# Gate and value by seven block products on 768 tokens, in three passes over combined weights

## The chip, the cores and the metric

The kernel runs on one core of one Trainium2 chip. The metric is the device time of one execution in microseconds. The engines are named as in the profile: PE (TensorE, matrix products), DVE (VectorE), ACT (ScalarE), POOL (GpSimd) and SP (SyncE, which here issues most transfers). SBUF is the memory on the chip that the engines work in, PSUM the small memory into which PE adds up its products.

## What is computed

```python
# attention without softmax over positions: B=8, H=8, S=576, D=64, 128 features
def phi(x):
    proj = einsum('bhsd,df->bhsf', x, w_phi)
    proj = proj - max(abs(proj), axis=-1, keepdims=True)
    return concatenate([exp(proj), exp(-proj)], axis=-1)
q_p, k_p = phi(q), phi(k)
kv = einsum('bhsf,bhsd->bhfd', k_p, v);  z = sum(k_p, axis=2)
attn = einsum('bhsf,bhfd->bhsd', q_p, kv) / (einsum('bhsf,bhf->bhs', q_p, z)[..., None] + 1e-06)
x = attn.transpose(0, 2, 1, 3).reshape(4608, 512)
# RMS norm, then gate and value (512 -> 1536), then output (1536 -> 512)
xn = x / sqrt(mean(x * x, axis=-1, keepdims=True) + 1e-06) * rms_g
g = xn @ w_gate;  val = xn @ w_val
out = (g * (1.0 / (1.0 + exp(-g))) * val) @ w_out
```

The weights of gate, value and output come in 64-bit floating point and are decoded on the chip; all else is 32-bit.

## The kernel before

A product of 32-bit numbers is made of three: each operand is split into a high part (a cast on ACT to the type that PE takes, `fp32r`) and a low part (a subtraction on DVE or POOL, `_split`, lines 59 to 61), and high x high, high x low and low x high are added up in PSUM. So every operand of a product costs one cast and one subtraction, and most rows on DVE and POOL at line 61 are such subtractions; their names end in `l`, those of the casts in `h`.

The program runs in three stages, one after the other, with some overlap.

- Attention (to about 512 us of the profile) handles pairs of heads in a software pipeline, and writes the tokens of x to `xs` in the chip's main memory. In its pauses PE does *fill* units (line 474): the products of the first three (`J1`) of the twelve blocks of 128 hidden columns with tokens that are not yet normalised, since the norm is a factor of each token that can be multiplied in later. One unit is 12 matmuls of 128x288; there are 96, and their results are stored in `gvs`. Units that attention did not take run behind it.
- The gate and value stage (about 620 to 1066 us) works on blocks of 384 tokens, 12 of them (`NB`), and for each on the nine other hidden blocks (`JN`). `gv` (line 576) makes 12 matmuls of 128x384 for the gate into `fp` and 12 for the value into `gp` (line 588); `hidden` applies the silu on ACT and multiplies on DVE (line 573) and stores to `hs`. All weights stay in SBUF, split (`wg`, `wv`, and `fg`, `fv` for the fills). Beside it `prep` makes the norm of the next block (squares on ACT, sums on POOL, line 151, the reciprocal and the scaling on DVE, lines 160 and 162, the split of x into `xb`), `gv_raw` scales the fills' results by the norm (line 596), 24 pieces of `w_out` are decoded (lines 47 to 55), and `load_o` splits weights of the output stage.
- The output stage (1066 us to the end) already uses Strassen's scheme in Winograd's form: the product of two by two blocks with seven block products instead of eight. It runs in 18 groups of 256 tokens, 126 matmuls of 128x256 each (line 742, `omm`). `load_o` makes the seven weight combinations of each of six weight groups (`kp`) and splits them into `wh`, `wl`; `operands` makes the seven token combinations of the next group (`a11`, `a12`, `s1` to `s4`, `a22`) while PE works on the present one.

The order of instructions on each engine is set when the program is built, by a scheduler that orders by data dependencies and priorities; each engine runs its own list in order. Pieces of side work are put between matmuls by hand in the Python loops. Tiles are reused in turn, so an instruction that writes a tile waits for the readers of what stood there.

## Time and profile before

| what | value |
|---|---|
| median of 3 runs | 1335.12 us (1331.82 to 1335.24) |
| span of the profiled execution | 1337.6 us |
| PE, DVE, ACT, POOL busy | 1288.5, 885.0, 711.0, 605.5 us |
| moved by DMA | 197.22 MB, mean 147 GB/s |
| matmuls 128x384 of the gate and value stage | 2592 |

The times are device times of whole executions. The profile is of one further execution; an engine is busy while one of its instructions runs. The stages are told apart by the source lines of PE's matmuls: 474 for fills, 588 for gate and value, 742 for output.

### The profile page before, as it was taken

What the parts mean: (1) busy time and instruction counts of PE and PEld (TensorE: products, weight loads), DVE (VectorE), ACT (ScalarE), POOL (GpSimd) and SP (SyncE); (2) the same over time, 40 slices, a digit from 0 to 9 for tenths busy, and PEclk for the clock granted to TensorE, in tenths of its full rate; (3) what the DMA queues carried; (4) which work ended last, traced back from release to release, by engine and by line L of the source; (5) the groups of instructions that cost most, each with busy time, mean ns of one, the idle gap of its engine ahead of it and who ended that gap; (6) DMA issues with size and microseconds to landing.
All of it is one profiled execution on the core that took longest, in us unless ns stands there. A gap on an engine that the chain in (4) does not pass through costs nothing.

```text
span 1337.6 us, 25479 instructions
## 1 busy us (share of the span) xinstructions
PE 1288.5 (96%) x9396; PEld 1275.6 (95%) x9396; DVE 885.0 (66%) x1301; ACT 711.0 (53%) x1510; POOL 605.5 (45%) x568
## 2 busy tenths in 40 slices
PE   7989999999999896899999999999999999999998
PEld 7989899999999896899999999999999999999998
DVE  7899788778778773313456656655534498777784
ACT  5988877778778782434344344443333334434332
POOL 3766565555555570000233223233221078788684
PEclk9999999999999898999999999999999999999999
DMA  5555556566555434843454454554433534554451
GB/s 159 127 147 156 161 158 165 167 170 169 157 164 161 123 95 127 249 153 126 141 170 140 157 168 133 166 168 140 133 115 108 183 111 126 150 166 127 142 168 54
DMA packets 204524, 197.22 MB, mean 147 GB/s; under 512 B 69552, under 2 KB 186416, under 8 KB 204400
## 3 DMA queue, kind: packets, MB, share of 16 engines
q1 hardware_dynamic: 186448, 181.44, 45.2%
q10 hardware_dynamic: 17952, 14.16, 3.8%
q8 instruction: 74, 1.21, 0.4%
q14 instruction: 50, 0.41, 0.1%
HBM read 126.04 MB, written 69.50 MB: 146 GB/s over the span
## 4 chain that ended last, share of the span: by engine, by line
PE 57%; DMA 3%; DVE 1%; ACT 0%; issue 0%; POOL 0%; ACTq 0%; SPq 0%; DVEq 0%
PE fp L588 17%; PE gp L588 16%; PE gd L742 6%; PE gz L742 6%; PE gy L742 5%; PE fp L474 4%; PE fp L742 3%; DMA wc<-wvs 1%; DMA gvs<-fo 1%; DMA rc<-di 0%; PE sm L415 0%; DMA dd<-nd 0%; ACT fo L477 0%; POOL s2l L61 0%; DVE a12l L61 0%
## 5 line engine op out<-in xcount | busy, mean ns | idle before, releaser
L380 POOL TENSOR_TENSOR ql<-eq,qh 128x256 fp32r<-128x256 f32 x256 | 217.7, 882 | 67.3 <-issue 39.5
L588 PE MATMUL gp<-xb,wv 128*128 128x384 f32 x864 | 161.9, 334 | 0.8 <-ACT wv L60 0.8
L588 PE MATMUL fp<-xb,wg 128*128 128x384 f32 x864 | 161.0, 334 | 0.0
L573 DVE TENSOR_TENSOR h<-sl,gp 128x384 f32<-128x384 f32 x108 | 59.6, 552 | 144.2 <-PE gp L588 75.6
L588 PEld LDWEIGHTS gp<-xb,wv 128*128 128x128 f32 x864 | 150.7, 188 | 1.0 <-ACT wv L60 1.0
L571 ACT ACTIVATE sl<-fp 128x384 f32<-128x384 f32 x108 | 52.8, 489 | 185.6 <-PE fp L588 170.7
L588 PEld LDWEIGHTS fp<-xb,wg 128*128 128x128 f32 x864 | 150.7, 188 | 0.0
L54 POOL TENSOR_TENSOR wa<-raw,wa 128x192 f32<-128x192 f32 (+1 forms) x112 | 66.2, 613 | 162.2 <-issue 58.6
L351 PE MATMUL acc<-vm,ek 128*128 128x65 f32 x1024 | 131.8, 271 | 0.0
L315 DVE TENSOR_REDUCE mx<-pp 128x4 f32<-128x512 f32 (+1 forms) x160 | 100.6, 632 | 43.0 <-PE pp L313 41.5
L351 PEld LDWEIGHTS acc<-vm,ek 128*128 128x128 f32 x1024 | 128.1, 195 | 0.4 <-ACT ek L338 0.4
L151 POOL TENSOR_TENSOR ss<-ss,sq 128x384 f32<-128x384 f32 x36 | 37.6, 1044 | 160.6 <-ACT sq L150 160.6
L61 POOL TENSOR_TENSOR xb<-x,xb 128x1536 fp32r<-128x1536 f32 x12 | 42.5, 3540 | 132.3 <-ACT xb L60 124.6
L474 PE MATMUL fp<-xo,fg 128*128 128x288 f32 x576 | 92.8, 302 | 5.7 <-ACT fo L477 3.4
L376 ACT ACTIVATE qh<-sm 128x512 fp32r<-128x512 f32 (+1 forms) x192 | 97.3, 507 | 0.0
L474 PE MATMUL fp<-xo,fv 128*128 128x288 f32 x576 | 92.2, 300 | 4.4 <-ACT fo L477 4.4
L311 PE MATMUL pp<-wh,th 128*128 128x256 f32 x288 | 89.0, 310 | 2.7 <-DVE yr L318 2.1
L474 PEld LDWEIGHTS fp<-xo,fg 128*128 128x128 f32 x576 | 81.7, 190 | 7.4 <-ACT fo L477 4.4
L474 PEld LDWEIGHTS fp<-xo,fv 128*128 128x128 f32 x576 | 81.7, 190 | 5.1 <-ACT fo L477 5.1
L61 POOL TENSOR_TENSOR s2l<-st,s2h 128x768 fp32r<-128x768 f32 x18 | 43.5, 2419 | 95.0 <-ACT s2h L60 47.6
L375 ACT ACTIVATE eq<-sm 128x512 f32<-128x512 f32 x128 | 78.4, 612 | 14.1 <-PE sm L364 13.2
L313 PE MATMUL pp<-wh,tl 128*128 128x256 f32 x288 | 83.0, 298 | 1.8 <-DVE tl L61 1.8
(198 smaller groups left out, 3801.8 us busy)
## 6 DMA issues: line engine op xcount, KB each, us to landing
hs<-h SPq DMA_DIRECT2D x144, 192.0 KB
ht<-hs SPq DMA_DIRECT2D x18, 1536.0 KB
gvs<-fo SPq DMA_DIRECT2D x96, 144.0 KB
gvr<-gvs SPq DMA_DIRECT2D x36, 384.0 KB
rc<-di SPq DMA_DIRECT2D x32, 288.0 KB
x<-xs ACTq DMA_DIRECT2D x16, 576.0 KB
x<-xs SPq DMA_DIRECT2D x12, 768.0 KB
kt<-in_k_dram SPq DMA_DIRECT2D x32, 256.0 KB
```

The source lines that it names most:

```text
L54: nc.gpsimd.tensor_tensor(a[:, h], lf[:, h], a[:, h], ALU.mult)
L61: (lo_eng or nc.vector).tensor_tensor(lo, x, hi.bitcast(F32), ALU.subtract)
L311: nc.tensor.matmul(o, th[:, cs], wh, start=True, stop=False)
L313: nc.tensor.matmul(o, tl[:, cs], wh, start=False, stop=True)
L315: nc.vector.tensor_reduce(mx[:, 0:2 * m], pp[:, 0:2 * m], axis=AX.X, op=ALU.max, apply_absolute_value=True)
L351: nc.tensor.matmul(acc[:, sg, h], e[h][:, sg, j], vm[:, h, j], start=False, stop=(h == 1 and j == T0 - 1))
L375: nc.scalar.activation(ei[:, sg], yi, AF.Exp, scale=1.0 - 2.0 * sg)
L376: nc.scalar.activation(hi[:, sg], yi, AF.Exp, scale=1.0 - 2.0 * sg)
L380: nc.gpsimd.tensor_tensor(lo[:, sg, cs], ei[:, sg, cs], hi[:, sg, cs].bitcast(F32), ALU.subtract)
L474: nc.tensor.matmul(fp[:, 0:TF], w, xx[x][:, c], start=(i == 0), stop=(i == 3 * NC - 1))
L588: nc.tensor.matmul(gp[:, 0:T], w, e[:, c], start=(i == 0), stop=(i == 3 * NC - 1))
L742: nc.tensor.matmul(place[n], a[:, kp], w[:, o], start=(first and kp == 0 and i == 0), stop=(kp == KP - 1 and i == 2), skip_group_check=True)
```

## The change

Gate and value are put on the seven-product scheme. The left matrix has two rows of blocks, gate and value, and two columns, the halves of the 512 inner columns; the right matrix has the two halves of the inner columns and two blocks of 384 tokens. So one *pair* (`pair`) serves 768 tokens and one hidden block j with 7 products x 2 inner blocks x 3 = 42 matmuls of 128x384 (line 666 of the changed kernel) instead of 48. Several products are added up in the same PSUM bank (`gx` or `fp`, `gy`, `gz`); five additions on DVE that read PSUM (line 670) combine the rest.

- The tokens need seven combinations, split, for each 768 tokens (`load_x`), and the weights seven for each j (`load_w`). The split token combinations are large, so only two blocks of 768 are held (`xa`), and only four sets of weights (`wb`, `NW`). The stage therefore runs in three passes (`NS`) of two blocks, and in each pass all nine weight sets are loaded and split again; the first pass computes the combinations and stores them in `wcs`, the other two load them.
- Norms are made in pieces (`norm`) for each 384 tokens. The fills' results are scaled in `raw`, six at the end of attention on DVE, the others on POOL in the first two passes.
- Side work stands in two lists, `todo` and `soon`, of which `step` runs pieces between the products.
- The 24 decodings of `w_out` stand in the third pass. `load_o` moves as a whole behind the gate and value stage, and the first output group is computed weight group by weight group.
- The fills' weights lie in attention's memory, so all fills end before the stage begins, but for what overlaps at its edge.

The diff, cut to the parts that are spoken of:

```diff
+    def norm(hb):
+        d = {}
+        def square(c):
+            sq = xm.tile([128, T], F32, name="sq" if c else "ss")
+            nc.scalar.activation(sq, xin[hb][:, c], AF.Square)
+            if c == 0:
+                d["ss"] = sq
+            else:
+                nc.gpsimd.tensor_tensor(d["ss"], d["ss"], sq, ALU.add)
...
+            sh = xm.tile([128, T], F32R, name="sq")
+            sl = xm.tile([128, T], F32R, name="sl")
+            _split(nc, sh, sl, d["ss"], lo_eng=nc.gpsimd)
+            nc.tensor.matmul(sp, ones, sh, start=True, stop=False)
+            nc.tensor.matmul(sp, ones, sl, start=False, stop=True)
+            ris[hb] = xm.tile([128, T], F32, name="ri", bufs=2)
+            nc.scalar.activation(ris[hb], sp, AF.Sqrt, scale=1.0 / DM, bias=eps)
+        def inverse(c):
+            nc.vector.reciprocal(ris[hb][:, c:c + 128], ris[hb][:, c:c + 128])
+        def scaled(c):
+            x = xin[hb][:, c]
+            nc.vector.scalar_tensor_tensor(x, x, g[:, c:c + 1], ris[hb], ALU.mult, ALU.mult)
...
-                nxt = prep(0, x0, ps_f, "fp")
+                for p in norm(0) + norm(1):
+                    p()
...
+            eng.tensor_tensor(d["r"], d["r"], ris[hb].unsqueeze(1).broadcast_to([128, 2, T]), ALU.mult)
+        def done():
+            r = d["r"]
+            nc.scalar.activation(r[:, 0], r[:, 0], AF.Silu)
+            nc.vector.tensor_tensor(r[:, 0], r[:, 0], r[:, 1], ALU.mult)
+            nc.sync.dma_start(out=hsv[:, j, at], in_=r[:, 0])
...
+            for p in raw(n, j, lambda: wk.tile([128, 2, 512], F32, name="eq")[:, :, 0:T], nc.vector):
+                p()
...
-            gp = ps_g.tile([128, 512], F32, name="gp") if wi else ps_f.tile([128, T], F32, name="fp")
...
+    PG = 3
+    SB = 2
+    NS = NB // (2 * SB)
+    SG = JN // PG * SB
+    NW = 4
...
+    def load_w(n, a, t):
+        d = {}
+        def begin():
+            pool = wlast if n % NW == NW - 1 else wpool
+            d["w"] = wb[n] = pool.tile([128, 2, 7, 256], F32R, name=f"wb{n % NW}")
+        def combos():
+            sub = lambda o, x, y: nc.vector.tensor_tensor(o, x, y, ALU.subtract)
+            nc.vector.tensor_tensor(t[:, 0], a[:, 2], a[:, 3], ALU.add)
+            sub(a[:, 2], a[:, 0], a[:, 2])
+            sub(t[:, 1], t[:, 0], a[:, 0])
+            sub(t[:, 2], a[:, 1], t[:, 1])
+            nc.sync.dma_start(out=wcv[n][:, 0:4], in_=a)
+            nc.sync.dma_start(out=wcv[n][:, 4:7], in_=t)
+        def split(x, os, lo_eng):
+            _split(nc, d["w"][:, 0, os], d["w"][:, 1, os], x, lo_eng=lo_eng)
+        return ([combos] if n < JN else []) + [begin, lambda: split(a, slice(0, 4), nc.gpsimd),
+                                               lambda: split(t, slice(4, 7), nc.vector)]
...
+    def load_x(bk):
+        d = {}
+        b11, b12, b21, b22 = (xin[2 * bk + i][:, 2 * k:2 * k + 2] for k in range(2) for i in range(2))
+        sub = lambda o, a, b: nc.vector.tensor_tensor(o, a, b, ALU.subtract)
+        def combos():
+            d["x"] = ops[bk] = xops[bk % SB].tile([128, 2, 7, 2, T], F32R, name="xa")
+            d["t"] = t = [xtp.tile([128, 2, T], F32, name=f"t{i}") for i in range(2)]
+            sub(t[0], b12, b11)
+            sub(t[1], b22, t[0])
+            sub(b12, b22, b12)
+        def split(i, x, lo_eng):
+            _split(nc, d["x"][:, 0, i], d["x"][:, 1, i], x, lo_eng=lo_eng)
+        def fourth():
+            split(4, d["t"][0], nc.vector)
+            sub(d["t"][0], b21, d["t"][1])
+        return [combos, lambda: split(0, b11, nc.gpsimd), fourth, lambda: split(5, d["t"][1], nc.vector),
+                lambda: split(1, b21, nc.gpsimd), lambda: split(6, d["t"][0], nc.vector),
+                lambda: split(3, b22, nc.gpsimd), lambda: split(2, b12, nc.gpsimd)]
...
+    def pair(bk, j, w, behind, step):
+        x = ops[bk]
+        X = ps_f.tile([128, T], F32, name="fp") if j % 2 else ps_g.tile([128, 512], F32, name="gx")[:, 0:T]
+        Y, Z = (ps_g.tile([128, 512], F32, name="g" + n)[:, 0:T] for n in "yz")
+        place = {1: X, 2: X, 6: Y, 7: Y, 4: Y, 5: Z, 3: Z}
+        def mm(n):
             i = 0
-            pl = place(wi, j)
-            for c in range(NC):
-                a, al = pl[0][:, c], pl[1][:, c]
-                for w, e in ((a, xh), (a, xl), (al, xh)):
-                    nc.tensor.matmul(gp[:, 0:T], w, e[:, c], start=(i == 0), stop=(i == 3 * NC - 1))
+            for c in range(2):
+                for a, e in ((0, 0), (0, 1), (1, 0)):
+                    nc.tensor.matmul(place[n], w[:, a, WSIDE[n], c * 128:(c + 1) * 128], x[:, e, XSIDE[n], c],
+                                     start=(i == 0 and n in (1, 6, 5)), stop=(i == 5), skip_group_check=True)
                     i += 1
-            r.append(gp[:, 0:T])
-        hidden(bk, J1 + j, *r)
-    def gv_raw(bk, j):
-        r = wk.tile([128, 2, T], F32, name="gvr", bufs=1)
-        nc.sync.dma_start(out=r, in_=gvv[j][:, :, bk * T:(bk + 1) * T])
-        nc.vector.tensor_tensor(r, r, xb[bk][2].unsqueeze(1).broadcast_to([128, 2, T]), ALU.mult)
-        hidden(bk, j, r[:, 0], r[:, 1])
-    W11, W21, W22, WT1, WT2, WT3, WT4 = range(7)
+        add = lambda o, a, b: nc.vector.tensor_tensor(o, a, b, ALU.add)
+        s1 = wk.tile([128, T], F32, name="s1")
+        vr = wk.tile([128, 2, T], F32, name="vr")
+        u, h = (wk.tile([128, T], F32, name=n) for n in "uh")
+        first = lambda: tc.high_priority(AHEAD)
+        with first():
+            mm(1)
+            nc.scalar.copy(s1, X)
+        step()
+        with first():
+            mm(6)
+            add(u, Y, s1)
+        step()
+        with first():
+            mm(5)
+        step()
+        for piece in behind:
+            with first():
+                piece()
+            step()
+        with first():
+            mm(2)
+            nc.scalar.activation(h, X, AF.Silu)
+        step()
+        with first():
+            mm(7)
+            add(vr[:, 1], Y, s1)
+            add(vr[:, 1], Z, vr[:, 1])
+        step()
+        def fourth():
+            mm(4)
+            add(vr[:, 0], Y, s1)
+        def third():
+            mm(3)
+            add(u, Z, u)
+            nc.scalar.activation(u, u, AF.Silu)
+            nc.vector.tensor_tensor(vr[:, 0], vr[:, 0], h, ALU.mult)
+            nc.vector.tensor_tensor(vr[:, 1], vr[:, 1], u, ALU.mult)
+            nc.sync.dma_start(out=hsv[:, J1 + j, 2 * bk * T:2 * (bk + 1) * T], in_=vr.rearrange("p a t -> p (a t)"))
+        return fourth, third
...
+    decs = [keep_o(i, j * 128, i * CH) for j in range(NJ) for i in range(DM // CH)]
...
+    for t in range(NS * SG):
+        s, u = divmod(t, SG)
+        gi, b = divmod(u, SB)
+        bk = s * SB + b
+        new = []
+        if t == 0:
+            new += raws(2) + raws(3)
+        if s and u == 0:
+            new += load_x(bk + 1)
+        if s + 1 < NS:
+            hb = 2 * SB * (s + 1) + u - 1
+            if u < SG - 2:
+                new.append(lambda hb=hb: get(hb + 1))
+            if 0 < u < SG - 1:
+                new += normed(hb) + raws(hb)
+            elif u == SG - 1:
+                new += load_x((s + 1) * SB)
+        for i in range(PG):
+            j = gi * PG + i
+            n = s * JN + j
+            togo[0] = 7 * (PG - i)
+            behind = pair(bk, j, wb[n], behind, step)
+            for up in done:
+                if up < NS * JN:
+                    soon += load_w(up, *wf.pop(up))
+                if up + 2 < NS * JN:
+                    soon.append(lambda up=up: wf.update({up + 2: fetch_w(up + 2)}))
+            done = [n + NW] if b == SB - 1 else []
+            if i == 0:
+                todo += new
+            if s == NS - 1 and decs:
+                soon += decs.pop(0)
+    for p in behind:
+        p()
+    run(soon + todo + sum(decs, []))
...
-    def load_o(kp, pool):
-        w, t = (rg.tile([128, 4, DH], F32, name="wc", bufs=2) for _ in range(2))
...
+    def load_o(kp):
+        w = rg.tile([128, 4, DH], F32, name="wc")
+        t = rg.tile([128, 3, DH], F32, name="wt")
+        for r, os in ((0, (W11, WT3)), (1, (W21, W22))):
             r0 = (2 * kp + r) * 128
             for k, o in enumerate(os):
                 nc.sync.dma_start(out=w[:, o], in_=wos[r0:r0 + 128, k * DH:(k + 1) * DH])
-        sub = lambda o, a, b: nc.vector.tensor_tensor(t[:, o], a, b, ALU.subtract)
-        sub(0, w[:, 3], w[:, W11])
-        sub(2, w[:, W22], w[:, 3])
-        sub(1, w[:, W22], t[:, 0])
-        sub(3, w[:, W21], t[:, 1])
-        wh = pool.tile([128, 7, DH], F32R, name=f"wh{kp}")
-        wl = pool.tile([128, 7, DH], F32R, name=f"wl{kp}")
-        _split(nc, wh[:, 0:3], wl[:, 0:3], w[:, 0:3])
-        _split(nc, wh[:, 3:7], wl[:, 3:7], t)
+        sub = lambda o, a, b: nc.vector.tensor_tensor(o, a, b, ALU.subtract)
+        sub(t[:, 0], w[:, WT3], w[:, W11])
+        sub(w[:, WT3], w[:, W22], w[:, WT3])
+        sub(t[:, 1], w[:, W22], t[:, 0])
+        sub(t[:, 2], w[:, W21], t[:, 1])
+        wh = owp.tile([128, 7, DH], F32R, name=f"wh{kp}")
+        wl = owp.tile([128, 7, DH], F32R, name=f"wl{kp}")
+        _split(nc, wh[:, 0:4], wl[:, 0:4], w)
+        _split(nc, wh[:, 4:7], wl[:, 4:7], t)
...
-    PRE = 4
...
-            if not decs and len(wos_ops) < PRE and n % 4 == 2:
-                wos_ops.append(load_o(len(wos_ops), rg))
...
+    wos_ops = [load_o(kp) for kp in range(KP)]
...
+        if gi == 0:
+            for kp in range(KP):
+                for n in (1, 2, 6, 7, 5, 3, 4):
+                    omm(n, n in (1, 2, 7, 3), [kp])
```

Three places show how the instructions stand. The first is DVE in the middle of the gate and value stage. Before, `h<-sl,gp` is the product of silu and value, `gvr` are fills' results, `wp` and `wa` belong to a decoding, and `ri` and `x` to a norm:

```order
851 L160 RECIPROCAL ri<-ri 128x384
852 L162 SCALAR_TENSOR_TENSOR x<-x,g,ri 128x384 x4
853 L596 TENSOR_TENSOR gvr<-gvr,ri 128x768
854 L573 TENSOR_TENSOR h<-sl,gp 128x384 x2
855 L50 TENSOR_SCALAR wp<-wa 128x256
856 L51 SCALAR_TENSOR_TENSOR wp<-wa,wp 128x256
857 L52 TENSOR_SCALAR wa<-wp 128x256
858 L55 TENSOR_TENSOR wa<-wp,wa 128x256
859 L573 TENSOR_TENSOR h<-sl,gp 128x384
```

After, near the end of the second pass, `vr` and `u` are the combinations out of PSUM, `wb` the low part of a weight set, `t` a fill's result:

```order
1058 L166 RECIPROCAL ri<-ri 128x128 x3
1059 L670 TENSOR_TENSOR vr<-gy,s_11286 128x384
1060 L670 TENSOR_TENSOR u<-gz,u 128x384
1061 L170 SCALAR_TENSOR_TENSOR x<-x,g,ri 128x384 x4
1062 L708 TENSOR_TENSOR vr<-vr,h 128x384
1063 L670 TENSOR_TENSOR vr<-gy,s_11371 128x384
1064 L60 TENSOR_TENSOR wb_11451<-wt,wb_11451 128x768
1065 L670 TENSOR_TENSOR u<-gz,u 128x384
1066 L709 TENSOR_TENSOR vr<-vr,u 128x384
1067 L554 TENSOR_TENSOR t_11533<-t_11533 128x384
```

One instruction that reads PSUM for each (384 tokens, j) has become five for each (768 tokens, j), with the products `vr<-vr,h` and `vr<-vr,u` besides, and splits of weights stand between them.

The second place is ACT at the step to the output stage. Before, `sl<-fp` are silus of the last gate products, `wh` casts of output weights, and `a11h` and the like casts of the first group's tokens:

```order
1179 L60 CAST wh_13263<-wc 128x1024
1180 L571 ACTIVATE sl<-fp 128x384
1181 L60 CAST wh_13279<-wc 128x768
1182 L571 ACTIVATE sl<-fp 128x384
1183 L571 ACTIVATE sl<-gvr 128x384
1184 L60 CAST wh_13279<-wc 128x1024
1185 L571 ACTIVATE sl<-fp 128x384 x3
1186 L571 ACTIVATE sl<-gvr 128x384
1187 L571 ACTIVATE sl<-fp 128x384 x3
1188 L571 ACTIVATE sl<-gvr 128x384
1189 L571 ACTIVATE sl<-fp 128x384
1190 L60 CAST a11h<-ht 128x768
```

After:

```order
1276 L692 ACTIVATE h<-gx 128x384
1277 L59 CAST wh_13305<-wc 128x1024
1278 L59 CAST wh_13305<-wt 128x768
1279 L59 CAST wh_13321<-wc 128x1024
1280 L59 CAST wh_13321<-wt 128x768
1281 L59 CAST a11h<-ht 128x768
1282 L59 CAST a12h<-ht 128x768
1283 L59 CAST a22h<-ht 128x768
1284 L707 ACTIVATE u<-u 128x384
1285 L59 CAST s3h<-st 128x768
1286 L59 CAST s1h<-ht 128x768
1287 L59 CAST s2h<-st 128x768
```

The casts of the weights, which stood among the silus of the gate stage, now stand behind all but the last of these and among the casts of the first group's tokens; eight more casts of weights follow.

The third place is PE where the fills end and gate and value begin. Before, the first matmuls of line 588 stand among fills, with many units still to come:

```order
2541 L474 MATMUL fp<-xo,fv_75 128x288
2542 L474 MATMUL fp<-xo,fv_74 128x288 x2
2543 L474 MATMUL fp<-xo,fv_75 128x288
2544 L474 MATMUL fp<-xo,fv_74 128x288 x2
2545 L474 MATMUL fp<-xo,fv_75 128x288
2546 L588 MATMUL gp<-xb,wv_2_8802 128x384
```

After, the last fill unit is followed by a norm's sum (`ones`) and the products of the first weight set:

```order
2829 L479 MATMUL fp<-xo,fv_118 128x288
2830 L479 MATMUL fp<-xo,fv_117 128x288 x2
2831 L479 MATMUL fp<-xo,fv_118 128x288
2832 L160 MATMUL fp<-sq,ones 128x384
2833 L161 MATMUL fp<-sl,ones 128x384
2834 L666 MATMUL gx<-xa,wb_8880 128x384 x6
```

The fills that were mixed with the first 36 matmuls of the stage now stand ahead of nearly all of them.

More of the change, by code (lines that the diff above doesn't have):

```diff
@@ L246, in decode_jobs @@
                     keep(jobs, src, dst, c * 128, c0, 384)
[L247 to L250 removed]
+        return jobs
     def decode_pieces(jobs, dec):
@@ new lines, with step @@
+    run(load_w(0, *wf.pop(0)))
+    run(load_x(0))
+    wf[2] = fetch_w(2)
+    run(normed(2))
+    run(load_w(1, *wf.pop(1)))
+    wf[3] = fetch_w(3)
+    run(normed(3))
+    run(load_w(2, *wf.pop(2)))
+    wf[4] = fetch_w(4)
+    run(load_w(3, *wf.pop(3)))
+    wf[5] = fetch_w(5)
+    run(load_x(1))
+    def step():
+        togo[0] -= 1
+        if soon:
+            soon.pop(0)()
+        for _ in range(-(-len(todo) // max(1, togo[0]))):
+            if todo:
+                todo.pop(0)()
```

206 lines of the change are left out of this document (94 added, 112 removed).

## Prediction

> **What bounds the kernel now.** I read the busy totals first, then a table of stretches, then the chain of waits inside each stretch, and last the timeline of single instructions on DVE and POOL. The totals:
>
> ```profile
> span 1337.6 us, 25479 instructions
> PE 1288.5 (96%) x9396; PEld 1275.6 (95%) x9396; DVE 885.0 (66%) x1301; ACT 711.0 (53%) x1510; POOL 605.5 (45%) x568
> ```
>
> PE is busy for 96% of the span, so fewer matmuls are worth time wherever PE is the one that is waited for. The stretches (PE, PEld, DVE, ACT, POOL busy, then the granted clock) say where that is:
>
> ```profile
> 500.00:560.00 60.00, 46.78 (x306) 45.08 (x305) 20.99 (x32) 21.87 (x46) 2.23 (x4) 0.91 0.66 193
> 560.00:616.00 56.00, 52.51 (x387) 51.34 (x386) 7.45 (x11) 21.30 (x49) 3.04 (x3) 1.00 0.43 141
> 900.00:1000.00 100.00, 100.00 (x579) 100.00 (x578) 50.81 (x74) 36.73 (x65) 26.64 (x23) 1.00 0.40 131
> 1064.00:1090.00 26.00, 23.14 (x188) 22.53 (x187) 23.15 (x15) 11.81 (x17) 20.76 (x9) 1.00 0.25 84
> 1090.00:1320.00 230.00, 230.00 (x1991) 229.82 (x1990) 181.25 (x160) 91.70 (x127) 177.38 (x81) 1.00 0.46 140
> ```
>
> The gate and value stage has PE full with DVE at half and POOL at a quarter: 49 us of DVE and 73 us of POOL are free per 100. The output stage has PE full too, but DVE and POOL at 79% and 77%. Only the end of attention and the step into the output stage have holes. The chain in the gate stage, in the fills ahead of it, in the attention's end, and in the step to the output stage:
>
> ```profile
> 525.42 6.23 DMA rc<-di
> ...
> 567.83 24.27 PE fp L474 x180
> ...
> 630.23 2.08 PE fp L588 x12
> 632.31 2.08 PE gp L588 x12
> ...
> 1064.61 2.10 PE gp L588 x12
> ...
> 1066.78 0.56 DVE h L573
> 1067.34 0.87 DVE a11l L61
> 1068.20 2.53 DVE a12l L61
> 1070.74 0.04 issue
> 1070.78 2.36 PE gy L742 x18
> ```
>
> Twelve matmuls of 128x384 take 2.08 us, 173.3 ns each. A fill unit (12 matmuls of 128x288) takes 24.27 / 15 = 1.62 us. The fourth stretch misses 2.9 us of PE around the step to the output stage. There DVE's 768-wide subtraction took 2.53 us, which leads to the view that matters most here, single instructions of DVE and POOL:
>
> ```profile
> 1072.39 2.57 POOL L61 TENSOR_TENSOR s1l<-ht,s1h 128x768 fp32r<-128x768 f32 x1
> 1073.17 2.61 DVE L61 TENSOR_TENSOR a11l<-ht,a11h 128x768 fp32r<-128x768 f32 x1
> 1074.91 2.57 POOL L61 TENSOR_TENSOR a22l<-ht,a22h 128x768 fp32r<-128x768 f32 x1
> 1075.70 2.60 DVE L678 TENSOR_TENSOR st<-ht 128x768 f32<-128x768 f32 x1
> ...
> 1153.20 0.95 DVE L61 TENSOR_TENSOR a11l<-ht,a11h 128x768 fp32r<-128x768 f32 x1
> 1156.68 1.84 POOL L61 TENSOR_TENSOR s3l<-st,s3h 128x768 fp32r<-128x768 f32 x1
> ...
> 679.60 3.49 POOL L61 TENSOR_TENSOR xb<-x,xb 128x1536 fp32r<-128x1536 f32 x1 [8.91 <-ACT xb L60]
> 680.94 0.55 DVE L573 TENSOR_TENSOR h<-sl,gp 128x384 f32<-128x384 f32 x1 [1.27 <-ACT raw L49]
> ```
>
> Alone, the DVE operation takes 0.95 us and the POOL one 1.84. Side by side each takes 2.6, and each ends some 0.8 (DVE) or 1.75 us (POOL) after the other ended: they take turns. One of each costs 2.52 us (start to start, 1072.39 to 1074.91). The DVE operation with a PSUM input (`h<-sl,gp`) runs through a POOL operation in 0.55 us. So POOL's work and DVE's work with only SBUF inputs add up to one load, which I call the turn-taking load and set against PE.
>
> **The change part by part.**
>
> *Matmuls removed.* For 768 tokens and one j, 48 matmuls become 7 products x 2 x 3 = 42. 54 such pairs: 2592 becomes 2268, and 324 x 173.3 ns = **-56.2 us**. Fills, attention and output keep their counts.
>
> *DVE and POOL work added.* The rows that price it, groups first and one instruction last:
>
> ```profile
> L573 DVE TENSOR_TENSOR h<-sl,gvr 128x384 f32<-128x384 f32 x36 | 20.1, 558 | 0.1
> L162 DVE SCALAR_TENSOR_TENSOR x<-x,g,ri 128x384 f32<-128x384 f32 x48 | 27.0, 624 | 0.5
> L151 POOL TENSOR_TENSOR ss<-ss,sq 128x384 f32<-128x384 f32 x36 | 37.6, 1044 | 160.6 <-ACT sq L150 160.6
> L61 POOL TENSOR_TENSOR fo<-ss,sq 128x384 fp32r<-128x384 f32 x12 | 13.1, 1091 | 25.3 <-DMA gvs<-fo 19.0 <-ACT sq L60 6.3
> L55 DVE TENSOR_TENSOR wa<-wp,wa 128x256 f32<-128x256 f32 x24 | 10.2, 426 | 24.2 <-POOL wa L54 24.2
> L61 DVE TENSOR_TENSOR wl<-wc,wh 128x1024 fp32r<-128x1024 f32 x6 | 7.3, 1222 | 0.6 <-ACT wh L60 0.5
> L61 DVE TENSOR_TENSOR wl<-wc,wh 128x768 fp32r<-128x768 f32 x6 | 5.7, 952 | 0.0
> L54 POOL TENSOR_TENSOR wa<-raw,wa 128x128 f32<-128x128 f32 x48 | 22.0, 479 | 98.2 <-issue 53.9 <-ACT sl L571 40.9 <-DVE wa L52 3.4
> ```
> ```profile
> 683.75 0.29 DVE L52 TENSOR_SCALAR wa<-wp 128x256 int32<-128x256 int32 x1
> ```
>
> Net of turns I take 0.55 us for 384 columns on DVE (0.5 back to back), 0.87 for 768 and 0.42 for 256; on POOL 1.04 for 384, 1.77 for 768 (2.52 less about 0.8), and for 1024 an estimate, 1.77 x 4/3 = 2.36. Per pass of 18 pairs:
> - products: two multiplications, 18 x 1.0 = 18. The five additions per pair read PSUM and take no turns.
> - raw blocks (POOL 768, DVE 384: 2.32 each): 18 in the first pass, 12 in the second, none in the third: 41.8, 27.8, 0.
> - norms of four 384-token blocks (POOL 3 x 1.04 + 1.09, DVE 4 x 0.55 = 6.4): 25.6, 25.6, 0.
> - token sums and splits (4 POOL x 1.77 + 7 DVE x 0.87 = 13.2): two, two, one: 26.4, 26.4, 13.2.
> - weights (POOL 2.36 + DVE 0.87 = 3.2, in the first pass 1.7 more for four sums; the four loaded before the loop not counted): 37.3, 28.8, 16.
> - decoding of w_out, 24 pieces, now all in the last pass (two POOL x 0.48 + two DVE x 0.42 + two x 0.29 = 2.4): 0, 0, 57.6.
>
> Sums: 149, 127 and 105 us, against 18 x 42 x 0.1733 = 131 us of PE a pass. So in the first pass this load is above PE. Nor is it level: in stretches of three pairs, in the order in which the program is written down, I count 32.1, 25.9, 29.2, 22.5, 17.2 and 27.1 us in the first pass and 24.5, 26.7, 12.9, 19.1, 15.3 and 29.6 in the second, against 21.8 us of PE (29.1 in the first stretch, where fills still run; up to 22.5 where norms stand). If PE could never run ahead, the excesses add up to 35 us. If it may run one pair (7.3 us) ahead of the load, 16 are left. With unlimited slack nothing is left by the end of the third pass. PSUM buffers give PE one pair, the four weight slots two or three, so one pair is the tightest and the nearest to how DVE's queue, which serves PSUM and splits in one order, will act: **+16**, bounds 0 and 45 (35 and 5% of the load lost in handing over).
>
> *Start of the stage.* The first gate matmuls were mixed with 41 fill units; now only four units are left then, and behind them PE waits for ACT's copy of the first product, which stands behind squares that wait for POOL's additions. Three of these and a table change: **+5**, bounds 0 (operands early) and 10.
>
> *End of attention.* The last of its holes and the cast that the next step needs:
>
> ```profile
> 507.82 0.61 PE L415 MATMUL sm<-qh,kv1l 128*128 128x288 f32 x1 [5.88 <-DVE kv1l L61]
> ```
> ```profile
> L60 ACT CAST wh<-wc 128x1024 fp32r<-128x1024 f32 x6 | 6.3, 1050 | 4.6 <-DVE wc L615 4.6
> ```
> ```profile
> 1091.18 4.16 PE gz L742 x36
> ```
>
> After the last attention matmul 60 fill units remain, against 52.5: 7.5 x 1.62 = 12 us no longer lie in attention's waits. The kv subtraction that held PE for 5.88 us stood on DVE behind the wait for the reciprocals (the transfer of 6.23 us above); it now stands ahead of it. 12 - 5.9 = **+6**, bounds 0 and 12.
>
> *Step to the output stage.* Before, all six weight groups were split under the gate matmuls. Now ACT's first cast of them waits for the last gate matmul (their memory is that of the gate weights). Behind it stand, on DVE, six subtractions of 1024 and of 768 (6 x 2.17 = 13.0) and the sums of four groups (16 x 0.42 = 6.7), besides the first group's own operands (7 x 0.87 on DVE, 5 x 1.77 on POOL = 14.9): 34.6 us by turns. The products now run weight group by weight group, so with the cast of 1.05 before and the 21 matmuls of the last weight group behind (2.4) the first output group ends 38 us after the last gate matmul. Its 126 matmuls take 14.6 (36 in 4.16 us), and the same step lost 2.9 before: 38 - 14.6 - 2.9 = 20.5, taken at **+20**; bounds 10 (DVE alone, POOL's part hidden) and 26 (the second group late too).
>
> *At nothing.* The third reading of combined weights adds some 25 MB over 400 us, 62 GB/s on 131; the DMA share there was 0.40, so it fits behind PE. ACT's casts rise to some 243 us of 400 and lie beside PE. If ACT's in-order queue holds a PSUM copy behind a silu that waits for POOL, that is part of the 16.
>
> Sum: -56.2 + 16 + 5 + 6 + 20 = -9, so 1328.4 for the profiled span of 1337.6. That execution is 2.5 above the median of 1335.1; the same change on the median gives **1326 us**, its own range 1308 to 1341.
>
> [...]
>
> **The rivals.**
> - *Everything added is covered.* For it: in the output stage the turn-taking load fills the time (14.9 us of priced work in 14.56 us a group, so my prices are even a little high) and PE is at 230.00 of 230.00. Then the gate stalls are 3, start and tail 4, the step 15: -34, **1301 us**. Against: the output stage's load is level, this one is not.
> - *Slower: DVE becomes the bound of the gate stage.* All PSUM additions stand in DVE's queue among splits and products that wait for POOL's turns; when one waits 2.6 us, PE's next product in that bank waits with it. At 5% of 380 us lost and no slack: 45; start 8, tail 6, step 22: +25, **1360 us**. It decides once stalls of the gate stage pass 30 us. For it: the first pass's 149 against 131. Against: the third pass has 26 us to spare, and weights are four ahead.
> - *The clock.* Where PE had holes the clock was halved for a while:
>
> ```profile
> 449.90:460.10 10.20, 10.20 (x49) 10.20 (x49) 4.14 (x7) 4.85 (x12) 6.23 (x8) 0.50 0.39 117
> 504.50:511.30 6.80, 3.48 (x14) 3.48 (x15) 1.83 (x4) 0.99 (x2) 0.00 (x0) 0.50 0.18 56
> ```
>
> The second row holds the hole of 5.88 us. Ten us at 0.50 cost 5. Three such after new holes (start, first pass, step to the output) add 15 to my sum of -9: +6, **1341 us**. [...]
>
> **How the numbers follow.** Forecast 0.44, all covered 0.20, DVE-bound 0.28, clock 0.08. A difference under 0.3% (4 us) is about what a measurement of this kernel cannot tell from none. Of the forecast's range two thirds lie below 1331, a quarter within the band; so faster 0.29 + 0.20 = 0.49, same 0.11 + 0.03 = 0.14, slower 0.04 + 0.28 + 0.05 = 0.37. The range reaches to the middle of the two outer cases: 1300 to 1358.
>
> **What would show it.** Gate stage at 403 us of PE work between the last fill and the last gate matmul, and a length of 415 to 425; holes of PE in the first pass and the early second, released by DVE, none in the third; POOL and DVE rows of 768 near 2.5 us there; 35 to 40 us from the last gate matmul to the end of the first output group, with DVE `wl` rows in the chain. A step under 30 us, or a gate stage without holes, makes it the first rival; holes in all passes make it the second.

## The result, and the profile after

The changed kernel takes 1470.89 us (median of 4 runs, 1467.56 to 1473.13) against 1333.47 us in the same session: a ratio of 1.1034, 95% interval 1.1007 to 1.1061. It is 10% slower; 1326 was predicted, and 1300 to 1358 as the range. The totals of its profile:

```profile
span 1469.0 us, 25394 instructions
PE 1299.0 (88%) x9072; PEld 1257.7 (86%) x9072; DVE 1132.1 (77%) x1652; ACT 789.4 (54%) x1629; POOL 759.0 (52%) x637
```

324 matmuls fewer, and PE is busy 10 us longer; DVE has 247 us more, POOL 154. The stretches (columns as in the prediction) tell where the 131 us between the two profiles are:

```profile
615.00:1166.00 551.00, 452.90 (x2338) 428.70 (x2336) 450.48 (x655) 228.57 (x404) 244.23 (x161) 0.92 0.43 146
```
```profile
638.00:800.00 162.00, 131.67 (x670) 124.75 (x670) 148.43 (x192) 76.13 (x125) 90.07 (x49) 0.91 0.46 156
800.00:985.00 185.00, 152.09 (x768) 145.81 (x768) 153.72 (x194) 79.60 (x133) 86.18 (x46) 0.90 0.42 141
985.00:1166.00 181.00, 151.85 (x806) 142.28 (x804) 133.63 (x260) 61.89 (x127) 56.35 (x60) 0.96 0.44 148
1166.00:1221.00 55.00, 35.55 (x249) 32.97 (x249) 51.89 (x54) 26.32 (x35) 28.47 (x12) 0.83 0.32 105
```

The first row is the whole gate and value stage, 615.0 to 1166.0: 551 us with 403 us of matmuls at full pace (2292 of 128x384 at 173.3 ns and the last 46 of the fills at 133). Of the 148 lost, 98 are holes, times in which PE stands still (551.0 - 452.9), 63 of them; 50 lie in PE's busy time (452.9 - 403). About 30 of these 50 are the clock: in thirteen stretches, each in or behind holes of together 2.3 us or more, the granted clock was 0.50 (behind the holes of 3.52 us at 916.9 and of 3.31 us at 1012.6 it stayed at 1.00). At 0.50 a matmul of 128x384 took 320 ns (the median, start to start) against 173.3. PE was busy for 65 of their 87 us, and close to half of that is lost:

```profile
sum 86.86, PE 65.13 PEld 62.62 DVE 69.15 ACT 29.34 POOL 19.06; mean PE 5.01 PEld 4.82 DVE 5.32 ACT 2.26 POOL 1.47
```

The other 20 stand mostly at the edges of the holes, where a matmul's row is 0.34 us long and no next one starts 0.17 us after it.

Before, the gate and value work took 453 us (447.0 from 619.7 on and 6 us of its matmuls among the fills). After, without the 6 us of fills in it, it takes 545, which is 92 more: the 148 less the 56.2 of the matmuls removed. All three passes lose: cut after every 756 of PE's gate matmuls (131 us at full pace) they took 197.6, 183.2 and 170.2 us. The last one, where the prediction had the load by turns far below PE, has 29 us of holes in the 181 us of its row above. The rest: what stands ahead of the stage takes some 8 us longer (it begins 4.7 us earlier, but with 6 us of fills still to come, where before 6 us of gate matmuls had been done), and from the last gate matmul to the end it is 303.0 us against 270.9, 32 more.

What PE and DVE waited for inside the stage (total, times, longest):

```profile
PE gy L666 <- DVE vr L670: 37.5, 20, 8.1
PE gy L666 <- DVE u L670: 20.5, 11, 5.1
PE gz L666 <- DVE u L670: 13.0, 7, 3.6
PE gz L666 <- DVE vr L670: 12.3, 7, 4.7
```
```profile
DVE vr L670 <- DMA hs<-vr: 29.6, 11, 8.4
DVE x L49 <- ACT x L47: 20.7, 13, 3.7
```

PE waits for the additions that free its PSUM banks. DVE's own waits by semaphore are smaller: its largest are 29.6 us for stores of products and 20.7 for ACT's part of the decoding. Most of its lateness is inside its instructions, as the groups show (mean ns after the total):

```profile
L708 DVE TENSOR_TENSOR vr<-vr,h 128x384 f32<-128x384 f32 x54 | 52.1, 965 | 0.7
L170 DVE SCALAR_TENSOR_TENSOR x<-x,g,ri 128x384 f32<-128x384 f32 x48 | 50.1, 1102 | 0.0
L60 DVE TENSOR_TENSOR wb<-wt,wb 128x768 fp32r<-128x768 f32 x27 | 45.9, 1705 | 6.4 <-ACT wb L59 6.4
L670 DVE TENSOR_TENSOR u<-gz,u 128x384 f32<-128x384 f32 x54 | 29.5, 546 | 2.1 <-PE gz L666 2.1
```

The addition with an input in PSUM takes 546 ns, as before. The product of the same size with both inputs in SBUF takes 965, a scaling 1102, a split of 768 columns 1705 instead of 950.

That POOL is the reason can be read from the same trace, if the instructions of one kind are parted by whether a POOL instruction ran beside them. The product `vr<-vr,h` took 550 ns in the 26 cases without one and 1350 in the 28 with one; the split of `wb` 944 and 1992 ns; the addition `vr<-gy,s`, which reads PSUM, 549 and 545. Nor did all work with its input in SBUF alone become longer: a reciprocal took 919 and 913. Added up over the stage, DVE's instructions last 118 us longer than they do without POOL beside them.

One hole of PE in the timeline shows how this reaches it (the instructions of PE, ACT and SP in between are left out):

```profile
711.20 4.24 POOL L549 TENSOR_TENSOR t<-t,ri 128x768 f32<-128x768 f32 x2
711.57 2.19 DVE L709 TENSOR_TENSOR vr<-vr,u 128x384 f32<-128x384 f32 x1
713.68 4.49 DVE L170 SCALAR_TENSOR_TENSOR x<-x,g,ri 128x384 f32<-128x384 f32 x4
718.10 1.34 DVE L554 TENSOR_TENSOR t<-t 128x384 f32<-128x384 f32 x1
719.36 0.55 DVE L709 TENSOR_TENSOR vr<-vr,u 128x384 f32<-128x384 f32 x1
719.83 0.55 DVE L670 TENSOR_TENSOR u<-gy,s 128x384 f32<-128x384 f32 x1
720.43 5.10 PE L666 MATMUL gy<-xa,wb 128*128 128x384 f32 x18 [5.07 <-DVE u L670]
```

POOL scales two raw blocks, and sums of a norm follow (two POOL rows of 1.3 and 1.2 us, left out here). DVE's product, its four scalings, the product of a fill and another product of a pair take 8.3 us together, where they take about 4 without POOL beside them; only then comes the addition for which PE has stood 5.07 us.

### The profile page after: what moved, and what is told of

The parts are those of the page before. It is cut to its first block, busy times and chain, and to the rows that moved or that the text cites. A ratio compares the mean times of both kernels' runs of the same rounds, so it can differ in the third digit from the quotient of the medians.

```text
span 1469.0 us, 25394 instructions
## 1 busy us (share of the span) xinstructions
PE 1299.0 (88%) x9072; PEld 1257.7 (86%) x9072; DVE 1132.1 (77%) x1652; ACT 789.4 (54%) x1629; POOL 759.0 (52%) x637
## 4 chain that ended last, share of the span: by engine, by line
PE 25%; DVE 20%; DMA 8%; issue 5%; ACT 2%; POOL 1%; SPq 0%; ACTq 0%; DVEq 0%; POOLq 0%
PE gd L912 5%; PE gy L912 5%; PE gz L912 5%; PE fp L479 3%; DMA hs<-vr 3%; PE gy L666 3%; DVE x L170 3%; DVE vr L670 2%; PE fp L912 2%; DMA x<-in_moe_w_out_dram 2%; DVE vr L708 2%; DVE vr L709 2%; DVE u L670 2%; DVE ri L166 1%; DVE wb L60 1%
## 5 line engine op out<-in xcount | busy, mean ns | idle before, releaser
L666 PE MATMUL gy<-xa,wb 128*128 128x384 f32 x972 | 215.2, 362 | 58.9 <-DVE vr L670 37.5
L666 PEld LDWEIGHTS gy<-xa,wb 128*128 128x128 f32 x972 | 184.8, 205 | 73.5 <-DVE vr L670 45.7
L666 PE MATMUL gz<-xa,wb 128*128 128x384 f32 x648 | 142.8, 352 | 25.6 <-DVE u L670 13.0
L666 PEld LDWEIGHTS gz<-xa,wb 128*128 128x128 f32 x648 | 120.3, 199 | 31.5 <-DVE u L670 15.9
L549 POOL TENSOR_TENSOR t<-t,ri 128x768 f32<-128x768 f32 x30 | 60.8, 2036 | 91.5 <-DMA t<-gvs 70.1
L60 POOL TENSOR_TENSOR wb<-wc,wb 128x1024 fp32r<-128x1024 f32 x27 | 71.0, 2633 | 47.9 <-ACT wb L59 39.0
L670 DVE TENSOR_TENSOR vr<-gy,s 128x384 f32<-128x384 f32 x108 | 59.0, 548 | 46.9 <-DMA hs<-vr 29.6
L666 PE MATMUL gx<-xa,wb 128*128 128x384 f32 x360 | 84.1, 351 | 7.9 <-ACT s L677 4.8
L153 POOL TENSOR_TENSOR ss<-ss,sq 128x384 f32<-128x384 f32 x36 | 40.8, 1134 | 91.4 <-ACT sq L149 91.4
L60 POOL TENSOR_TENSOR xa<-x,xa 128x768 fp32r<-128x768 f32 x24 | 54.8, 2307 | 60.8 <-ACT xa L59 60.7
```

Of the source, the lines that this page charges most:

```text
L60: (lo_eng or nc.vector).tensor_tensor(lo, x, hi.bitcast(F32), ALU.subtract)
L666: nc.tensor.matmul(place[n], w[:, a, WSIDE[n], c * 128:(c + 1) * 128], x[:, e, XSIDE[n], c], start=(i == 0 and n in (1, 6, 5)), stop=(i == ...
L670: add = lambda o, a, b: nc.vector.tensor_tensor(o, a, b, ALU.add)
```

## The experiments

Where two times stand together, the second is the kernel before in the same session. The times of single runs are given with the stage's length, from the first to the last gate matmul, which repeats better than the whole while the order of instructions stays: in e7, which leaves the stage as it is, it was 551.4 against 551.0 us. The edits of this table change that order, since the scheduler sets it anew at each build. By e13 order alone can be worth some 29 us, so differences of 10 us or less show little here.

| run | edit | stage, us | against 551 | DVE, POOL busy in it |
|---|---|---|---|---|
| e1 | no POOL splits and scalings | 477.1 | -74 | 351, 67 |
| e10 | no low parts on DVE | 509.8 | -41 | 412, 235 |
| e2 | no arithmetic of the decoding | 530.5 | -20 | 424, 214 |
| e5 | product stores from ACT's queue | 540.5 | -10 | 446, 241 |
| e6 | e1, e2 and e5 together | 456.2 | -95 | 323, 41 |
| e14 | e6 and no low parts on DVE | 447.2 | -104 | 287, 41 |
| e9 | one more addition per pair, one input in PSUM | 555.9 | +5 | 472, 241 |
| e12 | the same size, both inputs in SBUF | 574.5 | +23.5 | 485, 245 |
| e13 | same work, side pieces not moved ahead | 516.8 | -34 | 438, 233 |

**e1: POOL's work taken out.**

```diff
-            eng.tensor_tensor(d["r"], d["r"], ris[hb].unsqueeze(1).broadcast_to([128, 2, T]), ALU.mult)
+            if eng is nc.vector:
+                eng.tensor_tensor(d["r"], d["r"], ris[hb].unsqueeze(1).broadcast_to([128, 2, T]), ALU.mult)
...
-            _split(nc, d["w"][:, 0, os], d["w"][:, 1, os], x, lo_eng=lo_eng)
+            if lo_eng is nc.gpsimd:
+                nc.scalar.copy(d["w"][:, 0, os], x)
+            else:
+                _split(nc, d["w"][:, 0, os], d["w"][:, 1, os], x, lo_eng=lo_eng)
...
+                    a, e = (0 if WSIDE[n] < 4 else a), (0 if XSIDE[n] < 4 else e)
                     nc.tensor.matmul(place[n], w[:, a, WSIDE[n], c * 128:(c + 1) * 128], x[:, e, XSIDE[n], c],
```

> The changed kernel, but in the gate and value stage POOL makes no low parts (24 of tokens, 27 of weights) and does not scale the 30 raw blocks; the matmuls take the high part twice in their place, so PE's, ACT's and DVE's instruction counts stay. Left out: these low parts and the scaling. Turns theory (DVE's instructions with SBUF inputs wait for POOL's): about 160 us of POOL leave the stage, DVE's 450 us busy fall to about 340, and the stage falls from 551 us to 430 to 460. Queue theory (PE waits because one DVE queue serves PSUM behind other work and behind waits for ACT and transfers, whatever POOL does): the stage stays above 510.

```profile
613.70:1090.80 477.10, 432.43 (x2338) 416.51 (x2336) 351.25 (x655) 224.65 (x404) 66.54 (x84) 0.96 0.51 169
```
```profile
L716 DVE TENSOR_TENSOR vr<-vr,h 128x384 f32<-128x384 f32 x54 | 31.6, 584 | 0.8
```

1397.05 us against 1333.61. With the same 655 instructions DVE is busy 351 us instead of 450: 99 us of its time were waits for POOL (the 118 us above are 18 here), and the product `vr<-vr,h` takes 584 ns instead of 965. The stage falls by 74, between the two expectations: POOL's low parts and scalings are half of the loss, and the other half is something else.

**e2 and e5: the decoding, and the stores.**

```diff
-            nc.sync.dma_start(out=raw.rearrange("p n t -> p (n t)"), in_=w_out[at].bitcast(I32))
-            nc.sync.dma_start(out=wos[at], in_=_decode(nc, None, raw, CH, (x[:, 2 * CH:3 * CH].bitcast(I32), x[:, 3 * CH:4 * CH])))
+            nc.sync.dma_start(out=raw.rearrange("p n t -> p (n t)"), in_=xs[0:128, 0:2 * CH].bitcast(I32))
+            nc.sync.dma_start(out=wos[at], in_=x[:, 0:CH])
```

> The changed kernel, but the 24 pieces of w_out are not decoded in the last pass: their transfers stay (the same bytes, from x), the arithmetic on ACT, DVE and POOL is left out. Queue theory: the last pass, 181 us in the changed kernel, falls by 25 to 40 us, since DVE waited 20.7 us there for ACT's part of the decoding and spent some 40 us on it. Turns theory: the load by turns was below PE in that pass even with the decoding (105 against 131), so it falls by less than 10. The passes before stay as they are in both.

1455.83 us; 20 us less in the stage, 19 of them in the last pass (151.3 us instead of 170.2). The last 181 us of the stage have 162.1 us of PE instead of 151.9:

```profile
968.50:1149.50 181.00, 162.10 (x877) 159.56 (x876) 122.87 (x186) 55.51 (x95) 40.78 (x17) 0.94 0.47 158
```

That is under the 25 to 40 of the queue theory and above the 10 of the other. It is the worth of the whole decoding, not of DVE's wait for ACT alone.

```diff
-            nc.sync.dma_start(out=hsv[:, J1 + j, 2 * bk * T:2 * (bk + 1) * T], in_=vr.rearrange("p a t -> p (a t)"))
+            nc.scalar.dma_start(out=hsv[:, J1 + j, 2 * bk * T:2 * (bk + 1) * T], in_=vr.rearrange("p a t -> p (a t)"))
```

> The changed kernel, but the 54 stores of the products (hs<-vr) are issued from ACT's queue instead of SP's. Store theory: SP issues in order, and a store stands behind loads that wait for POOL's and DVE's splits; DVE waited 29.6 us for these stores because vr has two buffers. With a queue of its own that wait goes, and the kernel falls by 20 to 35 us. Turns theory alone: DVE is held by POOL anyway and the wait is only replaced, less than 8 us gained. If ACT itself becomes late by waiting for DVE before each store: slower by up to 20.

1461.07 us against 1338.98. The stage is 10 us shorter: less than the 20 that the store theory asked for, more than the 8 of the turns theory, and no more than another order could make. DVE's wait for the stores fell from 29.6 to 15.3 us. In the changed kernel a store could stand behind another transfer on its queue, as at the stage's end (SPq rows are issues of transfers), where a 1.5 MB load of the output stage went ahead of it:

```profile
1149.10 1.66 SPq L882 DMA_DIRECT2D ht<-hs  x2
1151.14 3.50 SPq L710 DMA_DIRECT2D hs<-vr  x2
1161.15 0.56 DVE L670 TENSOR_TENSOR vr<-gy,s 128x384 f32<-128x384 f32 x1 [8.35 <-DMA hs<-vr]
1161.76 2.29 PE L666 MATMUL gy<-xa,wb 128*128 128x384 f32 x6 [8.12 <-DVE vr L670]
```

**e6 and e14: together.** The edits of e1, e2 and e5 (e6); and besides them no low part at all (e14: both splits only cast, and the matmuls read the high part).

> The changed kernel with the three edits together: no low parts and no scaling on POOL, no arithmetic of the decoding, and the stores of the products from ACT's queue (left out: those low parts, the scaling and the decoding). If these three causes make up the loss in the gate and value stage, the stage (551 us, 476 without POOL's work) comes down to 405 to 425, near its 403 us of matmuls at full clock. If DVE's single queue (the five additions, two products and its own splits per pair) holds PE by itself, it stays above 445.

1377.42 us. 95 us are back, nearly the sum of the three (105). The 456.2 us are above both bounds that I had set, 425 and 445: the three causes are not all of it, and by the expectation DVE's single queue still holds PE.

**e9 and e12: one more instruction, two kinds of input.** After `add(vr[:, 1], Y, s1)` of each pair stands, in e9, the same addition again, and in e12 a maximum of `vr` with itself.

```diff
             add(vr[:, 1], Y, s1)
+            add(vr[:, 1], Y, s1)
```
```diff
             add(vr[:, 1], Y, s1)
+            nc.vector.tensor_tensor(vr[:, 1], vr[:, 1], vr[:, 1], ALU.max)
```

> The changed kernel with one addition per pair done twice (vr<-gy,s, 0.55 us, reads PSUM; the same value is written again): 54 x 0.55 = 30 us more on DVE that take no turns with POOL. As I counted in the prediction (only the load by turns stands against PE, additions that read PSUM are free): less than 8 us more. If PE pays for DVE's whole queue, its additions and its waits for POOL in one line: 25 to 40 us more in the gate and value stage (551 us).

> The changed kernel with one instruction more per pair on DVE, at the place where e9 had its doubled addition and of the same size (vr<-vr, 128x384, maximum of a tile with itself, which leaves it as it is), but with both inputs in SBUF instead of one in PSUM. Turns theory (what DVE loses, it loses waiting for POOL): where e9's 54 cost 5 us, these 54 cost 0.55 each and a wait for POOL, 30 to 60 us. If place and length in DVE's queue are all that counts, they cost the same 5 us.

```profile
L697 DVE TENSOR_TENSOR vr<-vr 128x384 f32<-128x384 f32 x54 | 40.2, 744 | 0.5
```

1475.83 and 1497.68 us. 54 instructions of 0.55 us, 30 us in all, cost the stage 5 with an input in PSUM, and 23.5 with both inputs in SBUF, a little under the 30 to 60 expected. In e9 DVE's idle time in the stage fell by 17 us and its waits for POOL by 7: most of the added work ran while DVE would have stood or waited anyway. Both totals agree with the turns, and the 25 to 40 of the queue theory did not come. But the comparison is not clean. In both runs DVE's other instructions stand in another order too, and pass by pass the stage changed by +3, +9 and -7 us in e9 and by +10, +9 and +4 in e12. So these two totals alone do not refute that PE pays for the length of DVE's queue; what shows the turns are the durations with and without POOL, given above, and e1.

**e10: DVE's low parts taken out**, with the edit of e1 turned round (`nc.vector` for `nc.gpsimd`, `>= 4` for `< 4`).

> The changed kernel without the 45 low parts that DVE makes in the gate and value stage (27 of weights, 18 of tokens, 768 columns each; the matmuls take the high part in their place; POOL's stay). They would take 39 us alone and took 76 us there, the rest of it waiting for POOL. If DVE's queue as a whole holds PE: the stage falls from 551 us by 50 to 80, though POOL's work is all still there. If POOL's load is what counts, by itself: by less than 30.

```profile
616.20:1126.00 509.80, 440.62 (x2337) 424.92 (x2336) 412.33 (x614) 225.51 (x404) 234.59 (x161) 0.94 0.47 157
```

1432.76 us, in the stage between the two expectations. 39 us of turn-taking work on DVE (at its price alone) give back 41; in e1, some 150 us of POOL's work at the prediction's prices gave back 74. A common load, as I counted it, would price both alike. What PE pays here is, roughly, DVE's time: its own SBUF work about in full, POOL's as far as DVE waits for it.

**e13: the same work in another order.**

```diff
-        if soon:
-            soon.pop(0)()
-        for _ in range(-(-len(todo) // max(1, togo[0]))):
-            if todo:
-                todo.pop(0)()
+        with late():
+            if soon:
+                soon.pop(0)()
+            for _ in range(-(-len(todo) // max(1, togo[0]))):
+                if todo:
+                    todo.pop(0)()
```

`late()` holds a piece behind the instructions written ahead of it on ACT, DVE and POOL.

> The changed kernel, the same instructions, but the pieces of side work may not be moved ahead of the additions after which the program writes them, so that fewer of DVE's splits, reciprocals and scalings stand in a row. If runs of side work in a row (the reciprocals and four scalings of a norm took 2.6 and 4.5 us together) make PE wait, the stage falls from 551 by 25 or more; if the amount of work and turns alone set it, by less than 10.

```profile
1135.00:1178.00 43.00, 0.13 (x1) 0.13 (x1) 26.02 (x52) 14.76 (x25) 7.67 (x12) 0.53 0.52 165
```

1466.41 us, nothing won in all, but the stage falls by 34. Six of the 24 decodings then come behind it, and PE stands still for 43 us between the stages. By e2's 20 us for 24 pieces these six are worth about 5, so some 29 of the 34 come from the order, on DVE, ACT and POOL together.

> The changed kernel with no low parts at all in the gate and value stage, no scaling on POOL, no decoding, and the product stores from ACT's queue (all that left out; the matmuls, additions, products, norms and casts stay). If DVE's low parts and POOL's work are what is too much, the stage comes to 405 to 430 us and PE is near full; if not, there is another wait, and it stays at e6's 456.

```profile
617.40:1064.50 447.10, 416.45 (x2338) 407.39 (x2336) 286.78 (x518) 209.03 (x356) 40.86 (x36) 0.98 0.54 180
```

1373.13 us; the stage comes to 447.2, not to the 405 to 430 expected. 44 us are left with DVE at 64%: 31 of holes and 13 in PE's busy time, about half of these by the clock (0.50 for 17 us). PE waits there 9.3 us for casts of weights and 15 for additions, DVE 21.8 for its stores. What holds PE for these 44 us is open.

**e3, e4, e7, e8 and e11: the pace of a matmul.** In the chain of waits, 36 matmuls of 128x256 of the output stage took 4.16 us before; after, and in e11:

```profile
1228.12 4.32 PE gz L912 x36
```
```profile
1203.86 4.08 PE gz L744 x36
```

120.0 ns each after, at a granted clock of 1.00, with the same order of matmuls. Before, the weight groups 1 to 3 ran at 113.3 ns (mean start to start), group 5 near 120, and groups 0 and 4, which follow a group of the other kind, near 117. In the addresses of the built programs, groups 0 to 3 lay 192 bytes (modulo 256) above the stationary tokens (224 against 32), groups 4 and 5, and all six after the change, at the same offset (32). The first two runs put `gl.tile([128, 56], F32, name="pad")` and the same with 48 ahead of all left-hand tiles of the kernel before.

> The kernel before with 224 unused bytes per partition ahead of its left-hand tiles, nothing else. It tests why matmuls of 128x256 in the output stage take 113.3 ns with the weights of groups 0 to 3 and 120.0 ns with groups 4 and 5 before, and 120.0 ns with all six after. If the start address of the moving operand sets it, those of groups 4 and 5 (now at a multiple of 256 bytes) change their pace, and the gate matmuls of 128x384 (173.3 ns) do too: 160 to 167 ns, and the whole kernel falls by 20 to 90 us. If not (the place in SBUF, or something else), all stays at 1335.

> The kernel before with 192 unused bytes per partition ahead, so that the left-hand tiles start at 224 above a multiple of 256 bytes, as the fast weight groups 0 to 3 do. If that offset makes the fast pace: groups 4 and 5 run at 113.3 ns too, gate matmuls near 167 ns, 15 to 40 us less in all. If not: 1335, groups 4 and 5 at 120.0.

1340.55 and 1341.19 us against 1333.61; from the last gate matmul to the end it is 277.0 and 280.0 us instead of 270.9. In e4 the stationary operands came to the same offset as groups 0 to 3, and all six ran at 120.0; in e3, with 224 bytes between them, at 117.5 to 120.0. The gate matmuls stayed at 173 ns in both. So it isn't the start address of the moving operand alone that counts, as I had supposed: that of groups 0 to 3 did not move. Its distance from the stationary one was the next guess. The next two put `[128, 8]` floats ahead of each weight group, in the changed kernel (e7) and in the gate stage of the kernel before (e8).

> The changed kernel with 32 unused bytes ahead of each of the six weight groups of the output stage, so that the moving operands start 32, 64, 96, 128, 160 and 192 bytes (modulo 256) above the stationary ones instead of at the same offset. If the pace of a 128x256 matmul hangs on that difference, the six groups, which follow each other three matmuls at a time, run at different paces, with 192 at 113.3 ns as in the kernel before, against 120.0 everywhere in the changed kernel; the output stage falls by 5 to 20 us. If it hangs on the place in SBUF, all six stay at 120.0.

> The kernel before with 32 unused bytes ahead of the weights of each of the first six hidden blocks of the gate and value stage, so that their moving operand (the tokens) starts 224, 192, 160, 128, 96 and 64 bytes (modulo 256) above the stationary one; the last three stay at 0. If the difference sets the pace: 173.3 ns for those at 0, as low as 160 to 167 ns for some others, and a stage up to 20 us shorter. If not, all stay at 173.3.

In e7 each group has another distance from its neighbours' and runs at 116.7 to 118.9, 4.23 us for 36. The group at 192 bytes ran at 116.7, not at the 113.3 that I expected of it: a group's own distance did not settle its pace while its neighbours lay at others. From the last gate matmul to the end it is 299.6 us against 303.0, less than the 5 to 20 expected. In e8 twelve matmuls of 128x384 take 2.08 to 2.12 us: other distances are no better there, some are worse, and the stage is 449.5 us against 447.0. Last, 192 bytes for all six groups in the kernel before:

```diff
     owp = ctx.enter_context(tc.tile_pool(name="owp", bufs=1, reuse_waits="tile"))
+    owp.tile([128, 48], F32, name="pad")
...
     xol = ctx.enter_context(tc.tile_pool(name="xol", bufs=1, reuse_waits="tile"))
+    xol.tile([128, 16], F32, name="pad")
```

> The kernel before with weight groups 4 and 5 of the output stage moved by 192 bytes (and 64 unused bytes behind them), so that all six groups start 192 bytes above the stationary operands modulo 256; the order of instructions is the same. If that difference makes the fast pace: all six run at 113.3 ns instead of four (groups 4 and 5 at 116.7 and 120.0), an output group takes 14.28 instead of 14.56 us, and the kernel falls by 5 us (0.4%). If it is the place in SBUF: no change.

All six run at 113.3 ns, 4.08 us for 36, as expected of the distance; an output group takes the 14.28 us expected, and in the profile the time from the last gate matmul to the end falls from 270.9 to 267.5. The whole kernel: 1333.74 against 1335.61 us, ratio 0.9997, interval 0.9973 to 1.002. A gain of this size (0.4%) is not to be seen in the total.

## Why the prediction was wrong, point by point

*Matmuls removed, -56.2:* right. 2268 were run, at 173.3 ns where PE was not held.

*Stalls of the gate stage, +16 (0 to 45), and the start, +5:* this failed. Both together are 148. The start alone came out at its size, but by luck: PE waited 4.82 us for ACT's copy, and that copy stood behind the copy of a fill that waited 2.75 us for a store and behind a table load, not behind squares that wait for POOL.

```profile
630.88 0.40 ACT L482 COPY fo<-fp 128x288 f32<-128x288 f32 x1 [2.75 <-DMA gvs<-fo]
631.72 1.28 ACT L163 ACT_TABLE_LOAD   x1
633.90 0.47 ACT L677 COPY s<-gx 128x384 f32<-128x384 f32 x1
634.43 2.29 PE L666 MATMUL gx<-xa,wb 128*128 128x384 f32 x6 [4.82 <-ACT s L677]
```

The step that failed is "If it may run one pair (7.3 us) ahead of the load, 16 are left", and with it the count under it. The mechanism was named rightly: POOL and DVE take turns here, an addition that reads PSUM does not (without and with POOL beside it, the product took 550 and 1350 ns, the addition 549 and 545). But I added both engines' work to one load and compared it with PE in stretches of three pairs, as if only the excess could be late. The runs showed three things in its place. DVE pays for its own SBUF work and for POOL's where it waits, and its additions stand behind both in one queue: 74 us for POOL, 41 for its low parts, the two overlapping. The excess arises within single microseconds, where four scalings stand ahead of one addition (e13, about 29 us by the order), and PE, which is full between the holes, does not win it back. And in or behind thirteen groups of holes the granted clock was 0.50 and a matmul of 128x384 took 320 ns instead of 173.3: about 30 of the 148. Two waits were not in the sum at all, the stores of `vr` (10 by e5, weakly) and DVE behind ACT's part of the decoding in the last pass, which I had counted as load there but not as a wait (20 us by e2 for the whole decoding). And some 44 us are left without all of this (e14), with no cause shown.

Two sums of this part were also wrong: 35 us and 5% of 380 are 54, not 45 (45 comes out if only the stretches above PE lose the 5%), and the six stretches of the first pass add up to 154, not to 149. Neither would have come near 148. The 5% itself was an assumption that no run shows.

That POOL and DVE take turns was in the prediction; it was the cost in a full queue that I mis-sized.

*End of attention, +6 (0 to 12):* some +8 was measured.

*The step to the output stage, +20 (10 to 26):* +32, outside its bounds, though its mechanism held. The last weights were split at the time that was worked out, on the first cast that waits for the last gate matmul:

```profile
1166.01 1.04 ACT L59 CAST wh<-wc 128x1024 fp32r<-128x1024 f32 x1 [13.42 <-PE gz L666]
```
```profile
1199.47 1.23 DVE L60 TENSOR_TENSOR wl<-wc,wh 128x1024 fp32r<-128x1024 f32 x1 [0.32 <-ACT wh L59]
1202.96 0.68 DVE L926 TENSOR_TENSOR ro<-gy,os 128x512 f32<-128x512 f32 x1
```

The first group ended some 37 us after the last gate matmul (38 predicted): 37 - 15.1 - 2.9 = 19, and PE waited 3.15 us more for `s4h` of the second group. Another 9.5 are 17 groups at 15.12 instead of 14.56 us: the pace of the matmuls, which was in no term of the prediction.

*The rivals.* The one that ended slower, DVE as the bound of the gate stage, came true in its place and sign; its price was 45 + 8 where 148 came. "For it: the first pass's 149 against 131" was the smaller reason, "Against: the third pass has 26 us to spare" was wrong, since that pass took 39 us more than its matmuls. The clock was a rival of its own with 15 us; it was a part of this one with about 30. Of what I named to look for, the holes in all passes were the mark of the second rival, and they are there.

*The chances.* 0.37 stood on slower, but the slowest case that was worked out ended at 1360; nothing in the prediction reached 1471.

## What to carry to other kernels

Where one in-order engine frees PSUM for PE, do not add up loads over several units of work; write down for each addition what stands ahead of it in that queue, at its contended price, and compare with the slack in PSUM, here one pair. A scaling on DVE, which takes turns with POOL, took 1157 ns on the mean in the stage here and 606 without POOL beside it, 1.9 times as long; so ahead of time-critical work one may try to put such work on ACT, in fewer instructions, or in gaps that hold the longer time; none of these was tried here. Before a plan that takes an eighth of the matmuls off a PE that is at 100%, ask what it adds to the engine that empties PSUM: here DVE went from 54 to 82% of the stage, and PE from 100 to 82%.
